# Retention attention into a highway layer: a planner's order replaced by one written-out order of all engines

## The chip, the cores and the metric

The kernel runs on one core of a Trainium2 chip. The metric is the device time of one execution in microseconds; several runs are timed, and their median is given. A profile is one execution recorded by the hardware profiler. Engine names: PE is TensorE (matmul), DVE is VectorE, ACT is ScalarE, POOL is GpSimd, SP is the engine that issues most DMAs.

## The reference

Four sequences of 768 tokens, 8 heads of 64 dimensions. The attention has no softmax; it decays by a per-head `lam` and is computed here in blocks of 64 tokens:

```
intra = (q k^T * Dmask) v          Dmask[i,j] = lam^(i-j) for i >= j, else 0
inter = (q * lam^(i+1)) kv_state
out   = intra + inter
kv_state = lam^64 * kv_state + (k * lam^(63-j))^T v
```

The result, as x of 3072 tokens by 512 features, goes through a highway layer with two 512x512 weights:

```
H = relu(x w_h);  T = sigmoid(x w_t + b_t);  y = T*H + (1-T)*x
```

Inputs and output are float32.

## The kernel before

A tile n is 256 tokens of one sequence with all 8 heads, so there are N = 12 tiles, three to a sequence, each of two chunks b of C = 128 tokens. A partition holds two neighbouring tokens (j = 0, 1), so a loaded row piece is 512 bytes. Decay is split into powers by position: v is multiplied by lam^(-position) when it is cast to bf16 (`scale_v`, POOL), and what comes out of attention is multiplied by lam^(+position) (`decay`, DVE, with a table `pow_q` of 128 x 4 x 768 that ACT makes with eight Exp).

Per tile: `load` k, q, v (SP); `cast` k and q to bf16 (POOL) and `scale_v`; `trans`, 8 PE transposes each of k and q; `evac_k`, `evac_q` copy them from PSUM to SBUF (ACT), where `evac_q` puts even and odd tokens back in order; `scores`, 64x64 matmuls for two halves u; `mask` (DVE) multiplies by the triangle into bf16; `state` adds k^T v of a chunk to the running state in PSUM, and `evac_s` copies the state to bf16; `inter` multiplies q by the state and `intra` the masked scores by v, both into `o`; `decay` turns `o` into `xT`, features on partitions. Then the highway layer: `block` is a group of 8 matmuls of 128x128 by 256 tokens for h (w_h) or t (w_t), for a pair of feature blocks; `hmx` is relu(h) - x (DVE), `sigm` the sigmoid (ACT, into bf16 SBUF), `thmx` their product (DVE); `turn` transposes x and adds the product on PE, giving tokens on partitions; `evac_o` copies to SBUF (ACT) and `store` writes 256 KB per chunk (SP). The last tile goes through the highway layer chunk by chunk. The first tile is loaded and cast in two head halves.

What sets the order: every piece of work is a `Task` with an engine, a guessed duration and a key. `plan` runs a list scheduler over them at build time and emits the instructions in the order of its guessed start times; each engine then executes its own part in that order and waits by semaphores. PSUM: two banks for the scores, two for `o`, one for the state, and three that rotate under the tag "w" for everything else (`WB = 3`). The state tile holds each head's 64x64 in its half of the partitions, 256 wide. Weight loads are eight DMAs of 256 KB whose keys place them after tile 0's loads:

```
a = task("SP", 0.5, WA[w] - 0.1 + 0.01 * (w * KC + kc), lambda w=w, kc=kc: load_w(w, kc), size=0.70)
```

Of the kernel before, what the change touches and what calls it, by code (L numbers as in the profile page):

```python
# [10 lines left out]
I32 = mybir.dt.int32  # L11
# [4 lines left out]
class Tile:  # L16
    def __init__(self, tag, bufs):
        self.tag, self.bufs, self.users, self.writers, self.obj, self.old = tag, bufs, [], [], None, None


class Task:
    def __init__(self, emit, eng, dur, key, reads=(), writes=(), after=(), lat=0.08, size=0.0, mode=0, only=()):
        self.__dict__.update(eng=eng, dur=dur, emit=emit, key=key, lat=lat, size=size, mode=mode, only=only)
        self.reads, self.writes, self.after = list(reads), list(writes), list(after)
        self.start = self.done = None


def plan(tasks):

    for t in tasks:  # L30
        deps = list(t.after)
        for x in t.reads:
            deps += [w for w in x.writers if w in t.only] or x.writers
            x.users.append(t)
        for x in t.writes:
            deps += x.writers
            x.users.append(t)
        for x in t.writes:
            x.writers.append(t)
        t.deps = [d for d in deps if d is not t]  # L40
    rings = {}
    engines = {}
    for t in tasks:
        engines.setdefault(t.eng, []).append(t)
    for e in engines.values():
        e.sort(key=lambda t: t.key)
    free = {e: START.get(e, 0.0) for e in engines}
    last_mode = None
    dma_free, services = 0.0, []
    busy = []  # L50
    warm = [False]
    order = []
    live = {}
    turn = {}
    for t in tasks:
        for x in t.writes:
            if x.writers[0] is t and x.tag != "w":
                turn.setdefault(x.tag, []).append(x)

    def slot_time(t):  # L60

        at = 0.0
        for x in t.writes:
            if x.old is None and x.writers[0] is t:
                q = live.setdefault(x.tag, [])
                if x.tag in turn and turn[x.tag][0] is not x:
                    return None
                if len(q) >= x.bufs:
                    prev = q[len(q) - x.bufs]
                    for u in prev.users:  # L70
                        if u.done is None:
                            return None
                        at = max(at, u.done if u.eng != t.eng else u.done - u.lat)
        return at

    def ready(t):
        at = slot_time(t)
        if at is None:
            return None
        for d in t.deps:  # L80
            if d.done is None:
                return None
            at = max(at, d.done if d.eng != t.eng or d.eng == "SP" else d.done - d.lat)
        return at

    remaining = len(tasks)
    W = 3.413
    win_end, win_busy, clock = W, 0.0, 1.9
    while remaining:
        best = None  # L90
        for e, ts in engines.items():
            if not ts:
                continue
            cand = None
            fixed = e == "SP"
            seen = 0
            for t in ts:
                r = ready(t)
                if r is not None:
                    s = max(free[e], r)  # L100
                    if cand is None or s < cand[0] - 1e-9:
                        cand = (s, t)
                        if s <= free[e] + 1e-9:
                            break
                seen += 1
                if seen > 60:
                    break
            if cand and (best is None or cand[0] < best[0] - 1e-9):
                best = (cand[0], cand[1], e)
        if best is None:  # L110
            stuck = [(e, ts[0].key) for e, ts in engines.items() if ts]
            raise RuntimeError(f"stuck {stuck}")
        s, t, e = best
        engines[e].remove(t)
        for x in t.writes:
            if x.writers[0] is t and x.old is None:
                live.setdefault(x.tag, []).append(x)
                x.old = True
                if x.tag in turn:
                    turn[x.tag].pop(0)  # L120
        t.start = s
        d = t.dur
        if e == "PE":
            while s >= win_end:
                if win_busy > 0.8 * W:
                    clock = 1.0
                elif win_busy < 0.1 * W:
                    clock = 1.9
                win_end += W
                win_busy = 0.0  # L130
            d = d * clock + (0.1 if t.mode != last_mode else 0.0)
            last_mode = t.mode
            win_busy += d
        t.end = s + d
        free[e] = t.end
        t.done = t.end + t.lat
        if e == "SP":
            begin = max(dma_free, s + 1.4)
            if len(services) >= 2:
                free[e] = max(free[e], services[-2])  # L140
            services.append(begin)
            dma_free = begin + t.size
            t.done = dma_free + (1.6 if t.writes or not t.reads else 0.4)
        order.append(t)
        remaining -= 1
    order.sort(key=lambda t: t.start)
    return order


LAT = dict(PE=0.25, ACT=0.08, DVE=0.08, POOL=0.08, SP=0.0)  # L150
START = dict(PE=4.8, ACT=6.2, DVE=4.9, POOL=4.2, SP=0.75)
W_ENG = ["POOL", "DVE"] * 4
LA = 5
XB = 3
OB = 12
WB = 3
KQ, KK, KV, KI, KS, KF, KO, KST = 0.9, 0.8, 0.6, 0.45, 0.5, 1.2, 1.8, 3.0
WA = (1, 1)
# [3 lines left out]
def kernel(  # L162
# [25 lines left out]

    def half(e):
        return slice(64 * e, 64 * e + 64)  # L190


    lam_bc = singles.tile([128, H], F32)
    nc.scalar.dma_start(out=lam_bc, in_=lam.partition_broadcast(128))
    bt_r = singles.tile([KC, 128], F32)
    nc.scalar.dma_start(out=bt_r, in_=moe_b_t.rearrange("(j p) -> j p", p=128))
    id128 = singles.tile([128, 128], BF16)
    make_identity(nc, id128)

    tri = singles.tile([128, J, C], F32)  # L200
    nc.gpsimd.memset(tri, 1.0)
    for b in range(2):
        nc.gpsimd.affine_select(out=tri[half(b)], in_=tri[half(b)], compare_op=ALU.is_ge, fill=0.0, base=0,
                                pattern=[[-1, J], [1, C]], channel_multiplier=-J)

    tk_i = singles.tile([128, NST, J], I32)
    nc.gpsimd.iota(tk_i, pattern=[[-2 * C, NST], [-1, J]], base=0, channel_multiplier=-J)

    tq_i = singles.tile([128, S], I32)
    nc.gpsimd.iota(tq_i, pattern=[[1, S]], base=0, channel_multiplier=0)  # L210
    ln_bc = singles.tile([128, H], F32)
    nc.scalar.activation(ln_bc, lam_bc, AF.Ln)
    ln_hp = singles.tile([128, NP], F32)
    for e in range(2):
        nc.scalar.activation(ln_hp[half(e), :], ln_bc[half(e)].rearrange("p (hp e) -> p e hp", e=2)[:, e, :], AF.Copy)
    tk_f = singles.tile([128, NST, J], F32)
    nc.vector.tensor_copy(tk_f, tk_i)
    tq_f = singles.tile([128, S], F32)
    nc.vector.tensor_copy(tq_f, tq_i)
    pk_ln = singles.tile([128, NST, H, J], F32)  # L220
    nc.vector.tensor_tensor(pk_ln, in0=ln_bc[:, None, :, None].to_broadcast([128, NST, H, J]),
                            in1=tk_f[:, :, None, :].to_broadcast([128, NST, H, J]), op=ALU.mult)
    pow_k = singles.tile([128, NST, H, J], F32)
    nc.scalar.activation(pow_k, pk_ln, AF.Exp)
    pow_q = singles.tile([128, NP, S], F32)
    id_f = singles.tile([KC, KC], F32)
    nc.vector.tensor_copy(id_f, id128[0:KC, 0:KC])
    bt_ps = ps.tile([128, KC], F32, tag="w", name="bt_ps", bufs=WB)
    nc.tensor.transpose(bt_ps, bt_r, id_f)
    bt_col = singles.tile([128, KC], F32)  # L230
    nc.vector.tensor_copy(bt_col, bt_ps)
    w_f = [singles.tile([128, KC, DM], F32, name=f"w_f{i}") for i in range(2)]
    w_b = [singles.tile([128, KC, DM], BF16, name=f"w_b{i}") for i in range(2)]
    wh, wt = w_b


    tasks = []
    made = {}

    def buf(name, tag, shape, dtype=BF16, bufs=1, pool=None):  # L240
        made[name] = Tile(tag, bufs)
        made[name].make = lambda: (pool or sb).tile(shape, dtype, tag=tag, name=tag, bufs=bufs)
        return made[name]

    def get(*key):
        x = made[key]
        if x.obj is None:
            x.obj = x.make()
        return x.obj
# [274 lines left out]
```

## Time and profile before

| what | value |
|---|---|
| time, median of 3 runs | 119.48 us (118.65, 119.48, 119.56) |
| profiled execution: span from first to last instruction | 118.0 us |
| profiled execution: time of its own beside the span | not given; the runs lie 0.6 to 1.5 us above the span |
| PE busy | 98.8 us |
| DVE busy | 81.1 us |
| ACT busy | 70.7 us |
| POOL busy | 52.3 us |
| granted PE clock | full in all slices |
| HBM read, written | 20.98 MB, 6.29 MB |

How to read it: the page gives busy time, then forty equal slices of the span in tenths, then the chain of work that ended last. A group line gives source line, engine, operation, output and inputs with shapes, count, busy time and mean duration, and the idle time before it with what released it. A matmul's listed duration holds its pipeline, so four that overlap each show some 220 ns; start to start is what counts.

### The profile page before, as it was taken

What the parts mean: (1) busy time and instruction counts of PE and PEld (TensorE: products, weight loads), DVE (VectorE), ACT (ScalarE), POOL (GpSimd) and SP (SyncE); (2) the same over time, 40 slices, a digit from 0 to 9 for tenths busy, and PEclk for the clock granted to TensorE, in tenths of its full rate; (3) what the DMA queues carried; (4) which work ended last, traced back from release to release, by engine and by line L of the source; (5) the groups of instructions that cost most, each with busy time, mean ns of one, the idle gap of its engine ahead of it and who ended that gap; (6) DMA issues with size and microseconds to landing.
All of it is one profiled execution on the core that took longest, in us unless ns stands there. A gap on an engine that the chain in (4) does not pass through costs nothing.

```text
span 118.0 us, 4685 instructions
## 1 busy us (share of the span) xinstructions
PE 98.8 (84%) x2049; PEld 83.0 (70%) x2049; DVE 81.1 (69%) x138; ACT 70.7 (60%) x135; POOL 52.3 (44%) x52
## 2 busy tenths in 40 slices
PE   0056548776899999999999999999988999999970
PEld 0044436565688878888888888888777888888950
DVE  0539461229768887969869788698698775988460
ACT  3599203393874665784677757837576578353860
POOL 7148432777585765864484647458360000000000
PEclk9999999999999999999999999999999999999999
DMA  0999999899999999999999999999912204004045
GB/s 17 267 304 380 366 294 284 234 252 305 289 293 272 301 290 290 305 300 322 335 290 315 304 265 300 300 315 263 314 64 89 94 0 173 10 6 178 6 178 177
DMA packets 42413, 27.57 MB, mean 234 GB/s; under 512 B 1301, under 2 KB 38425, under 8 KB 42393
## 3 DMA queue, kind: packets, MB, share of 16 engines
q1 hardware_dynamic: 42240, 27.27, 82.4%
q8 instruction: 16, 0.26, 1.0%
q14 instruction: 5, 0.03, 0.1%
q10 hardware_dynamic: 152, 0.01, 0.1%
HBM read 20.98 MB, written 6.29 MB: 231 GB/s over the span
## 4 chain that ended last, share of the span: by engine, by line
PE 67%; DMA 12%; DVE 7%; SPq 4%; issue 3%; ACT 2%; POOL 1%; DVEq 0%
PE w L367 33%; PE w L385 9%; DMA qf<-in_q_dram 8%; PE w L299 8%; PE s L317 6%; PE o L341 5%; DMA w_f<-in_moe_w_h_dram 4%; DVE th L379 4%; SPq L282 4%; PE kv L349 3%; PE o L330 3%; DVE m L321 2%; ACT L376 1%; POOL qb L286 1%; ACT t_sb L376 1%
## 5 line engine op out<-in xcount | busy, mean ns | idle before, releaser
L367 PE MATMUL w<-xT,w_b 128*128 128x256 bf16 (+1 forms) x416 | 49.0, 268 | 0.0
L367 PEld LDWEIGHTS <-w_b 128*128 128x128 bf16 x416 | 36.9, 99 | 4.6
L321 DVE TENSOR_TENSOR m<-s,tri 128x512 bf16<-128x512 f32 x48 | 31.6, 684 | 4.0 <-PE s L317 3.5
L376 ACT ACTIVATE t_sb<-w,bt_col 128x256 bf16<-128x256 f32 (+1 forms) x52 | 21.0, 458 | 18.6 <-PE w L367 17.1
L292 POOL TENSOR_TENSOR vs<-vf,pow_k 128x1024 bf16<-128x1024 f32 (+1 forms) x13 | 23.1, 1778 | 11.7 <-DMA vf<-in_v_dram 9.1
L355 DVE TENSOR_TENSOR xT<-o,pow_q 128x512 bf16<-128x512 f32 x24 | 15.4, 685 | 11.4 <-PE o L341 11.4
L371 DVE SCALAR_TENSOR_TENSOR hmx<-w,xT 128x512 bf16<-128x512 f32 (+1 forms) x26 | 16.7, 642 | 5.5 <-PE w L367 5.4
L286 POOL CAST qb<-qf 128x1024 bf16<-128x1024 f32 (+1 forms) x13 | 12.7, 979 | 16.4 <-DMA qf<-in_q_dram 13.9
L379 DVE TENSOR_TENSOR th<-t_sb,hmx 128x512 bf16<-128x512 bf16 (+1 forms) x26 | 15.8, 606 | 4.7 <-ACT t_sb L376 4.5
L391 ACT ACTIVATE o_sb<-w 128x512 f32<-128x512 f32 (+1 forms) x24 | 13.7, 588 | 7.3 <-PE w L385 7.3
L303 ACT ACTIVATE kT<-w 128x1024 bf16<-128x1024 bf16 (+1 forms) x13 | 12.4, 954 | 6.5 <-PE w L299 6.5
L308 ACT ACTIVATE qT<-w 128x1024 bf16<-128x1024 bf16 x11 | 11.3, 1024 | 7.4 <-PE w L299 7.4
L286 POOL CAST kb<-kf 128x1024 bf16<-128x1024 f32 x11 | 11.9, 1079 | 5.3 <-DMA kf<-in_k_dram 5.3
L385 PE MATMUL w<-id,th 128*128 128x128 bf16 x96 | 13.1, 219 | 0.6 <-DVE th L379 0.6
L385 PE MATMUL w<-id,xT 128*128 128x128 bf16 x96 | 13.2, 220 | 0.0
L317 PE MATMUL s<-qT,kT 64*64 64x128 bf16 x384 | 11.5, 229 | 1.5 <-DVE m L321 1.4
L349 PE MATMUL kv<-vs,kb 64*64 64x64 bf16 x320 | 9.2, 198 | 2.1 <-POOL vs L292 1.4
L349 PEld LDWEIGHTS <-kb 64*64 64x64 bf16 x320 | 7.6, 113 | 4.2 <-issue 4.2
L299 PE MATMUL w<-id,kb 128*128 128x128 bf16 x96 | 8.4, 235 | 2.5 <-POOL kb L286 1.9
L317 PEld LDWEIGHTS <-kT 64*64 64x64 bf16 x384 | 7.5, 110 | 3.9 <-DVE m L321 2.4
L385 PEld LDWEIGHTS <-th 128*128 128x128 bf16 x96 | 9.3, 98 | 1.1 <-DVE th L379 1.0
L385 PEld LDWEIGHTS <-xT 128*128 128x128 bf16 x96 | 9.1, 98 | 1.0
(37 smaller groups left out, 78.3 us busy)
## 6 DMA issues: line engine op xcount, KB each, us to landing
out_dram<-o_sb SPq DMA_DIRECT2D x23, 256.0 KB, 4.8
kf<-in_k_dram SPq DMA_DIRECT2D x11, 512.0 KB, 7.3
qf<-in_q_dram SPq DMA_DIRECT2D x11, 512.0 KB, 7.8
vf<-in_v_dram SPq DMA_DIRECT2D x11, 512.0 KB, 7.1
w_f<-in_moe_w_h_dram SPq DMA_DIRECT2D x4, 256.0 KB, 5.2
w_f<-in_moe_w_t_dram SPq DMA_DIRECT2D x4, 256.0 KB, 5.6
kf<-in_k_dram SPq DMA_DIRECT2D x2, 256.0 KB, 4.7
qf<-in_q_dram SPq DMA_DIRECT2D x2, 256.0 KB, 5.5
```

The source lines that it names most:

```text
L286: eng.tensor_copy(get(x + "b", n)[:, :, hs, :].rearrange("p j h d -> p h j d"), get(x + "f", n, p).rearrange("p h (j d) -> p h j d", j=J))
L292: eng.tensor_tensor(get("vs", n)[:, hs].rearrange("p h j d -> p (h j) d"), in0=get("vf", n, p).rearrange("p h (j d) -> p (h j) d", j=J), i ...
L299: T.transpose(get(x + "tr", n, p)[:, i, j, :], get(x + "b", n)[:, j, h:h + 2, :], id128)
L317: T.matmul(get("s", n, u)[half(b), e, i, j, :], lhsT=get("kT", n)[half(e), hp, j, half(b)], rhs=get("qT", n)[half(e), hp, b * C:(b + 1) * ...
L321: V.tensor_tensor(get("m", n, u)[:, e], in0=get("s", n, u)[:, e], in1=tri[:, None].to_broadcast([128, 2, J, C]), op=ALU.mult)
L349: T.matmul(get("kv", n // NST)[half(e), hp, :], lhsT=get("kb", n)[half(b), j, 2 * hp + e, :], rhs=get("vs", n)[half(b), 2 * hp + e, j, :], ...
L355: V.tensor_tensor(get("xT", g)[:, :, r * C:(r + 1) * C], in0=get("o", n)[:, b], in1=pow_q[:, :, c * C:(c + 1) * C], op=ALU.mult)
L367: T.matmul(get(x, g, js[0])[:, i, :], lhsT=w[:, kc, j * 128:(j + 1) * 128], rhs=get("xT", g)[:, kc, :], start=(kc == 0), stop=(kc == KC - 1))
L371: V.scalar_tensor_tensor(get("hmx", g, js[0]), in0=get("h", g, js[0]), scalar=0.0, in1=get("xT", g)[:, js[0]:js[-1] + 1, :], op0=ALU.max, ...
L376: A.activation(get("t_sb", g, js[0])[:, i, :], get("t", g, js[0])[:, i, :], AF.Sigmoid, bias=bt_col[:, j:j + 1])
L379: V.tensor_tensor(get("th", g)[:, js[0]:js[-1] + 1, :], in0=get("t_sb", g, js[0]), in1=get("hmx", g, js[0]), op=ALU.mult)
L385: T.matmul(get("x", n, b, p)[:, (j - js[0]) * 128:(j - js[0] + 1) * 128], lhsT=get(x, g)[:, j, r * C:(r + 1) * C], rhs=id128, start=(j == ...
```

## The change

The planner, its tasks and their guessed costs are removed. A string `PLAN` lists every step of every engine in one sequence; each token is a step with its tile, half and, where there is a choice, its engine after `@` and its PSUM bank or banks after `=` (seven single banks b0 to b6, the eighth for the state). The kernel walks the string and emits.

```
+PLAN = """
+Lq.0.0 Lq.0.1 Lq.1.0 Lk.0.1 Lv.0.1 Lk.0.0 Lv.0.0 Lk.1.0 CQ.0.1@POOL Lq.1.1 Lv.1.1 CQ.0.0@POOL CK.0.1@ACT Lk.1.1
+TQ.0.0=0 TQ.0.1=1 Lv.1.0 TK.0.1=2 EK.0.1@DVE CK.0.0@POOL Lq.2.1 CV.0.1@DVE TK.0.0=3 EQ.0.1@DVE CV.0.0@POOL Lk.2.0
...
+I.2=61 CQ.3.2@POOL Lk.4.1 X.1.1@DVE G.1.0@ACT A.2.0 A.2.1
+X.0.0@DVE Lv.4.0 TK.3.2=2 D.2.1@ACT H.1.0 R.0.1.2=5 EK.3.2@ACT Lk.5.1 CV.3.2@POOL TQ.3.2=0 X.1.0@DVE R.0.0.2=1 Lq.5.0
+EQ.3.2@ACT D.2.0@DVE R.1.1.2=3 R.1.0.2=4 Lk.5.0 E.0.1.2@ACT CQ.4.2@POOL SS.3.1=26 F.2.1.0=0 Lv.5.0 KE.3.0@ACT M.3.1.1
...
+"""
```

The tokens: L loads, W weight loads, C casts (CQ now a multiply), WC weight casts, T transposes, E with K or Q their copies out of PSUM, SS scores with state (S and U each alone, in tile 0), KE state copy, M mask, I inter, A intra, D output copy into `xT` (`take`), F highway matmuls, H relu, G sigmoid, X gate multiply, R turn, E output copy, ST store. What the steps do differently:

```
+    def cast_q(n, p, eng):
+        scale(n, p, eng, "qf", new(("qb", n), [128, J, H, D])[:, :, heads(p)].rearrange("p j h d -> p h j d"), pow_q)
...
+    def state(n, b, hp, j, e):
+        first = n % NST == 0 and b == 0 and hp == 0 and j == 0
+        T.matmul(kv[half(e), hp, half(e)], lhsT=get("kb", n)[half(b), j, 2 * hp + e, :],
+                 rhs=get("vs", n)[half(b), 2 * hp + e, j, :], start=first, stop=True, skip_group_check=True)
...
+    def scores_state(n, e, bk):
...
+        for i, (hp, j, x) in enumerate((hp, j, x) for hp in range(NP) for j in range(J) for x in range(2)):
+            score(n, e, hp, j, x)
+            if st:
+                state(n, b, *st[i])
...
+                    T.matmul(get("o", n, b)[:, hp, :], lhsT=get("ss", n, b)[:, hp, :],
+                             rhs=get("qT", n)[:, hp, :, half(b)],
+                             start=hp == 0, stop=False, skip_group_check=True)
...
+    def take(n, b, eng):
+        g, r = groups(n, b)
+        z = 2 if len(g) == 1 else 1
+        copy(eng, new(("xT", *g), [128, NP, z * C], tag=f"xT{z}")[:, :, r * C:(r + 1) * C].rearrange("p n (q j) -> p n j q", j=J),
+             get("o", n, b).rearrange("p n (j q) -> p n j q", j=J))
...
+        dst = src if place == "ACT" else new(("tb", g, u), [128, 2, z * C], tag=f"tb{z}")
```

In words. The query's decay power is multiplied in when POOL casts q, from a small table like v's; the 768-wide table and the multiply after attention go, and `take` is a plain copy on ACT or DVE. Tokens stay even-odd through q's copy, the scores, the mask and `o`, and `take` writes them back in order. Scores are made for one head parity e at a time and alternate with the state matmuls of the chunk on the other half of the rows. The state is 128 wide per head pair with zeros off its diagonal (one memset), so `inter` is one full 128x128 matmul per head pair and chunk, and the state copy is 512 wide. The sigmoid is written in place in PSUM and the gate multiply reads it there. Loads are all in head halves of 256 KB, and weights come as four DMAs of 512 KB, after most of tile 2. The sigmoid table is loaded ahead of its first use. All stores are from SP: 256 KB each, the last chunk's in two halves, as before. A step that keeps PE spinning (`Z`) is defined and not used.

## The prediction

> **What bounds the kernel now.** I read the page first: busy shares and the forty slices.
>
> ```profile
> PE 98.8 (84%) x2049; PEld 83.0 (70%) x2049; DVE 81.1 (69%) x138; ACT 70.7 (60%) x135; POOL 52.3 (44%) x52
> PE   0056548776899999999999999999988999999970
> DMA  0999999899999999999999999999912204004045
> ```
>
> From slice 12 on TensorE is full; before that it is half idle while the DMA engines are full. So there are two stages: a start of some 34 us that waits for data, then a stretch that TensorE sets. The chain of waits in order of time shows the end of the start:
>
> ```profile
> 11.18 9.08 DMA qf<-in_q_dram
> 20.31 1.05 POOL qb L286
> 21.41 1.05 PE w L299 x8
> 22.50 1.02 issue
> 23.52 1.28 ACT L376
> 24.81 0.85 ACT t_sb L376 x2
> 25.68 1.29 DVE th L379
> ```
>
> Tile 1's q lands only at 20.3 us, because all 2 MB of weights were queued before tile 1; then a table load of 1.28 us and a slow gate multiply stand on the path. The same chain in a full stretch prices TensorE's pieces:
>
> ```profile
> 55.78 0.55 PE w L299 x8
> ...
> 58.55 0.45 PE w L299 x8
> 58.99 0.87 PE w L367 x8
> 59.87 0.57 PE o L341 x32
> 60.44 0.24 PE kv L349 x16
> 60.68 1.85 PE w L367 x16
> ```
>
> Eight transposes take 0.45 us behind another 128-wide group and 0.55 behind a 64x64 one: a change of array shape costs about 0.1. In the trace four 64x64 matmuls on different quarters start 3 to 4 ns apart and the next four 56 ns later; a pair of state matmuls takes 32 ns; start gaps at a change of shape are about 93 ns longer. The waits and the gate's tile view show the rest:
>
> ```profile
> POOL qb L286 <- DMA qf<-in_q_dram: 13.9, 10, 3.7
> POOL vs L292 <- DMA vf<-in_v_dram: 9.1, 10, 2.0
> ...
> L379 DVE TENSOR_TENSOR th<-t_sb,hmx x26: 283/415/1724, 25.7 to 113.7; 128x512 bf16<-128x512 bf16 x22, 128x256 bf16<-128x256 bf16 x4
> ```
>
> GpSimd (Pool) idles for data; the gate multiply takes 415 ns at the median and up to 1724.
>
> **What the Trainium skill says.** "TensorEngine Tiling (Array Packing)", Key Properties: changing the tiling mode drains the engine. The 0.45 against 0.55 agrees. "SBUF — State Buffer", Who interferes with whom: a Vector instruction with two SBUF inputs shares a port with a Pool instruction that reads SBUF, and the later one waits. The spread 415 to 1724 agrees, as does the mask with one PSUM input, which stays within 673 to 692. "VectorE: DVE Perf Modes", perf-mode tier table: a copy from PSUM runs at up to 2x. No bf16 1024-element Vector copy is in this trace.
>
> **The change part by part.**
>
> *TensorE.* Units, from the spacings above: 8 transposes or 8 output-turn matmuls 0.45, 8 wide F matmuls 0.875, 16 scores 0.225 (four rounds), 32 intra 0.45, 16 state 0.256, 16 inter 0.45. A full tile before: F 3.5, transposes 0.9, turns 0.9, intra 0.45, scores 0.45, state 0.51, inter 0.45, and six changes of shape 0.56: 7.7. The chain's intra groups from 30.08 to 106.81 give 7.67 a tile. After: alternating takes a score pair on one row half and a state pair on the other, so a round of four costs 56 ns; 16 scores with 16 states take 0.45, two of those 0.90, against 0.96. Inter becomes 8 full-array matmuls of 56 ns, 0.45 as before. So alternation and block-diagonal state are worth next to nothing by themselves. The written order has 40 changes of shape where the trace has 68: 28 x 0.093 = 2.6 us saved. Summed over all tiles (the first of a batch has half an inter, the last half a state): 90.3 before, 88.2 after.
>
> *Start.* Loads are reordered: tiles 0 and 1 whole, most of tile 2, then weights in four 512 KB pieces between tile 2 and 3. Same bytes, 72 loads of 256 KB where there were 39. The trace lands the first six halves at 5.5 to 10 us and 6.5 MB by 27.3 (v of tile 2); I take 0.93 us per 256 KB and 1.4 per weight piece. Then tile 1 is complete at 15.5, v of tile 2 at 23.9, the last weights at 27.6, tile 3 at 32. Pool's order: the scaling of tile 2's v runs 23.9 to 25.8. The scores-and-state pair of tile 2 therefore ends at 26.9; the 12 us of TensorE work ahead of it fit well before. Then four F blocks 3.5, inter, intra, transposes and four turns of tile 0 and 1; Vector is as late (four masks 2.6, four gates 2.6, relu and copies to 34.1), and v of tile 3 is scaled at 34.1. Tile 3's scores start at 34.4. At that point 18.6 of the 88.2 are done, 69.6 remain. Before, at 34.1, 13.4 of 90.3 were done and 76.9 remained; it took until 114.4, 80.3: 3.4 of waits, 4%.
>
> *The rest of the start.* Eight Exp for the decay table (4.4 us of ScalarE) and its iota go; a memset of the state bank and a second 0.24 Exp come, and the sigmoid table is loaded early, off the path. All this lies beside the first loads: nothing; uncovered, under 1 us.
>
> *Pool.* q's cast (1046 ns) becomes a multiply like v's (1912): 12 x 0.87 = +10 us, 4.9 a tile against some 7 of TensorE, hidden behind the data waits above, which stood at 23. It is not hidden at tiles 2 to 4, where loads arrive every 5.6: included in 34.4; without that cover +0.9 a tile. Loads keep 4 to 7 us ahead of the transposes after tile 4 at 0.295 MB/us.
>
> *Stores.* 25 stores, 6.29 MB, as before: nothing in themselves. But on SP's fixed queue nine stand ahead of the last load, and the one of tile 3's first half is asked for at about 53.4, just when its turn is due: 0 to 2 us of loads held up, covered by that lead.
>
> *Vector and ScalarE.* Removed: 24 decay multiplies (685). Added: 24 output takes, 13 on ScalarE (0.6) and 11 on Vector (0.65 back to back, as the masks' 1.29 for two). State copies double to 512 wide: 0.38 to 0.6 on ScalarE; 10 of 20 go to Vector at 0.65. Eight whole transposed-tile copies go to Vector: unknown, from 0.66 (632 cycles at 0.96 GHz, an estimate from the named page, 2x) to 1.2 (1x; 128x512 with stride took 0.69); even-odd order makes them contiguous, so I take 0.68. Gates read the sigmoid in PSUM: 0.65 steady instead of 0.41 to 1.7; no port wait. Behind tile 3: masks 36 x 0.645, relu 18 x 0.645 + 4 x 0.4, gates the same, takes 5.9, transposed copies 4.0 (7.1 if slow), state copies 3.9, output copies 2.4: 65.5 us of Vector beside 69.6 of TensorE, 94%. Before, Vector had 63.4 in the 80 us from 35 to 115. This is where the gain will leak. Scores now wait for v too, since states stand between them, and state b=1 waits for its copy on a crowded Vector queue; behind a waiting scores pair stand masks, and behind those intra. Walking tiles 3 and 4 by hand I find 1.9 us of waits in 13.8 (mask and state copy behind relu and gates). I take 8% for the whole stretch, between 4% before and that 13%: 5.6 us.
>
> *Sum.* Start +0.3 (34.4 for 34.1), remaining work -7.3, waits +2.2, end from the last turn to the last store unchanged (3.85): 118.04 - 4.8 = 113.2 span. The page gives a span of 118.0 and no separate time of its execution; the median of the runs shown, 119.48, is 1.4 above it, the lowest 118.65 is 0.6. Carrying 1.4 gives 114.6; in proportion, 114.6.
>
> **The rivals.**
>
> A, faster still: waits at 2 to 3%, because port waits of the gate vanish and the order was written with all engines in view. 34.4 + 71.4 + 3.85 = 109.7, time 111.1. For: TensorE held 99.9% busy from 60 to 80 us before. Against: Vector's 94%.
>
> B, no change: the early order doesn't help. If the F blocks of tiles 0 and 1 start with the last weights and Vector or Pool lag, tile 3 starts at 38; with 10% waits 38 + 76.6 + 3.85 = 118.4, time 119.8. For: DMA is full from 2 us on in both. Against: bytes needed for tile 2 fit by 24.
>
> C, slower: Vector becomes the bound in fixed order. Place: tiles 3 to 11. Each tile TensorE waits w for a mask, state copy or gate queued behind others on Vector that are themselves not ready. The forecast has w = 0.6; from w = 1.35 the span passes 119.2 (the 1% line); at w = 1.6 it is 34.4 + 69.6 + 14.4 + 3.85 = 122.3, time 123.7. For: 94%, slow copies add 3 us; seven single PSUM banks named in advance can't be swapped. Against: ScalarE has only some 53 us in the same stretch, and the copies are split in detail.
>
> D: the alternation doesn't run four wide (row halves do not overlap): each scores-state pair costs 0.6 in place of 0.45, +3.3 us, 118 time. Scores across both row halves already overlap, so this is unlikely; it lies in the range.
>
> **How the numbers follow.** Forecast 0.52, A 0.20, B and D 0.12, C 0.16. About 1% is what a measurement of this kernel can tell from no change. Faster: forecast, A and some of B and D: 0.76; within 1%: 0.09; slower: C with a little of B and D: 0.15. The predicted time is the forecast's, 114.6. Range: low 109.5 (below A's centre, with a start 1 us earlier), high 121.0, into C, leaving about two in ten outside; the slow Vector copies and D's price fall within it.
>
> **What would show it.** Right: tile 3's first scores near 34 us, after F blocks of two tiles and four turns; 40 changes of shape; scores-state groups of 32 in about 0.45; the gate near 0.68 without long ones; whole Vector copies near 0.68; TensorE's small waits on Vector spread over tiles 3 to 11; last turn near 109.5. Wrong: TensorE idle over 1 us a tile on masks or state copies, Pool waits for data beyond tile 5, transposed copies of 1.2 on Vector, or a first F block much later than 20 us.

## The result and the profile after

The changed kernel took 111.95 us (median; 111.24 to 112.56) against 119.52 us for the kernel before: a ratio of 0.942, 95% interval 0.9345 to 0.9495, 5.8% faster. The ratio compares undisturbed executions only, so it is not the quotient of the two medians. The forecast was 114.6. The profiled execution took 111.24 us with a span of 109.5, the fastest of the four; the forecast span was 113.2.

The page of the changed kernel: busy time and share by engine, then tenths of 40 slices for TensorE, Vector and the DMA engines.

```profile
span 109.5 us, 4558 instructions
PE 95.4 (87%) x1969; PEld 84.8 (77%) x1969; DVE 84.0 (77%) x144; ACT 66.3 (61%) x120; POOL 60.8 (55%) x51
PE   0007887999999999999999999999999999999960
DVE  0204794739996699799999899899999968867870
DMA  0999999999999999999999999999955331020584
```

TensorE starts later than before (slice 4 instead of 3) and is full from slice 8 instead of slice 12. Vector, at nine tenths or more in 8 of 40 slices before, is there in 19 now.

The list of waits of the changed kernel, TensorE alone (microseconds in total, times, longest; gaps below 0.15 us are not listed), complete:

```profile
PE bqtr L205 <- POOL qb L191: 8.8, 2, 8.3
PE kv L222 <- ACT ss L103: 0.7, 1, 0.7
PE bktr L205 <- POOL kb L105: 0.6, 1, 0.6
PE bx L328 <- DVE th L319: 0.3, 1, 0.3
PE bs L217 <- DVE qT L105: 0.3, 1, 0.3
PE kv L222 <- DVE ss L105: 0.2, 1, 0.2
```

Of the first line 8.3 us are the time until the very first transposes. After 20 us TensorE waited once, for 0.3 us. Busy time in stretches, with the columns TensorE, its weight loads, Vector, ScalarE, Pool, clock, DMA share and GB/s:

```profile
20.00:36.00 16.00, 16.00 (x294) 13.95 (x289) 12.20 (x21) 9.81 (x17) 11.30 (x10) 1.00 1.08 300
36.00:60.00 24.00, 24.00 (x529) 21.04 (x522) 22.60 (x37) 16.21 (x30) 17.88 (x12) 1.00 1.10 306
60.00:80.00 20.00, 20.00 (x468) 17.99 (x465) 18.68 (x31) 12.59 (x23) 15.44 (x11) 1.00 1.08 324
```

Vector was 94% and 93% busy in the last two stretches, and TensorE has no listed wait in them. The gate multiply, in its tile view of the changed kernel (shortest, median, longest in ns):

```profile
L319 DVE TENSOR_TENSOR th<-bt,hm x26: 414/680/693, 30.2 to 105.5; 128x512 bf16<-128x512 f32 x22, 128x256 bf16<-128x256 f32 x4
```

Its longest went from 1724 to 693 ns. Marks on TensorE, in us from the first instruction, place the gain (start times in the two traces; these two executions lie 8.3 us apart, the ratio stands for about 7):

| mark | before | after | gain so far |
|---|---|---|---|
| 64th F matmul (two tiles' worth) | 38.7 | 31.6 | 7.1 |
| first scores of tile 3 | 39.1 | 35.6 | 3.5 |
| last intra of tile 5 | 60.2 | 55.5 | 4.7 |
| last intra of tile 8 | 83.3 | 78.4 | 4.9 |
| last turn | 114.2 | 106.1 | 8.1 |

Between tiles 5 and 8 both kernels go at about the same pace, 23 us for three tiles. The gain is made before 55 us, and again after 83. Of the 3.2 us after 83 only some 0.7 us are known waits: the kernel before stood 0.45 us at a gate of 1.67 us and 0.26 at a mask behind it. Most of the rest, about 2 us by the count of the next paragraph, is work that the changed kernel has already done at that mark, and fewer changes of shape.

Counted in the prediction's unit prices (an estimate), the kernel before has 71.9 us of TensorE work left at tile 3's first scores and takes 75.1 to its last turn; the changed kernel has 69.6 left and takes 70.5. So the 8.1 us are 3.5 at the start, 2.3 of less work behind it and 2.3 of fewer waits.

The chain of the changed kernel in order of time shows a stretch of the full part:

```profile
43.30 1.85 PE bt L301 x16
45.15 0.45 PE bo L272 x8
45.59 0.87 PE bh L301 x8
46.47 0.45 PE bktr L205 x8
46.91 0.87 PE bh L301 x8
47.79 0.45 PE bqtr L205 x8
```

Six groups stand in a row with the array in one shape (the inter group, L272, is now 128 wide too), and the eight transposes take 0.45 us both times; behind a 64x64 group they took 0.55.

### The profile page after: what moved, and what is told of

It is laid out like the page before. It is cut to its first block, busy times and chain, and to the rows that moved or that the text cites. A ratio compares the mean times of both kernels' runs of the same rounds, so it can differ in the third digit from the quotient of the medians.

```text
span 109.5 us, 4558 instructions
## 1 busy us (share of the span) xinstructions
PE 95.4 (87%) x1969; PEld 84.8 (77%) x1969; DVE 84.0 (77%) x144; ACT 66.3 (61%) x120; POOL 60.8 (55%) x51
## 4 chain that ended last, share of the span: by engine, by line
PE 80%; SPq 5%; DMA 5%; DVE 2%; POOL 2%; ACT 2%; issue 1%; DVEq 0%
PE bt L301 20%; PE bh L301 19%; PE bx L328 9%; PE bs L217 8%; PE bo L282 6%; PE bqtr L205 6%; SPq L173 5%; PE bktr L205 5%; DMA qf<-in_q_dram 5%; PE bo L272 5%; PE kv L222 2%; POOL qb L191 2%; DVE o L105 1%; ACT ss L103 1%; ACT o L103 1%
## 5 line engine op out<-in xcount | busy, mean ns | idle before, releaser
L256 DVE TENSOR_TENSOR m<-bs,tri 128x512 bf16<-128x512 f32 x48 | 31.0, 679 | 4.1 <-PE bs L217 3.9
L315 ACT ACTIVATE bt<-bt,bt_col 128x256 f32<-128x256 f32 (+1 forms) x52 | 22.0, 431 | 8.5 <-PE bt L301 5.6
L191 POOL TENSOR_TENSOR qb<-qf,pow_q 128x1024 bf16<-128x1024 f32 (+1 forms) x13 | 23.0, 1772 | 7.0 <-ACT pow_v L134 3.6
L301 PE MATMUL bh<-xT,w_b 128*128 128x256 bf16 (+1 forms) x208 | 25.1, 269 | 0.0
L191 POOL TENSOR_TENSOR vs<-vf,pow_v 128x1024 bf16<-128x1024 f32 (+1 forms) x12 | 22.0, 1835 | 5.5 <-DMA vf<-in_v_dram 5.5
L301 PE MATMUL bt<-xT,w_b 128*128 128x256 bf16 (+1 forms) x208 | 24.0, 265 | 0.0
L319 DVE TENSOR_TENSOR th<-bt,hm 128x512 bf16<-128x512 f32 (+1 forms) x26 | 16.6, 644 | 2.0 <-ACT bt L315 1.2
L306 DVE SCALAR_TENSOR_TENSOR hm<-bh,xT 128x512 bf16<-128x512 f32 (+1 forms) x26 | 16.2, 640 | 1.3 <-PE bh L301 1.3
L217 PE MATMUL bs<-qT,kT 64*64 64x128 bf16 x384 | 15.4, 233 | 0.3 <-DVE qT L105 0.3
L328 PE MATMUL bx<-id,th 128*128 128x128 bf16 x96 | 12.9, 219 | 0.3 <-DVE th L319 0.3
```

What stands on the lines that cost most here:

```text
L191: ENG[eng].tensor_tensor(dst, in0=get(src, n)[:, heads(p)].rearrange("p h (j d) -> p h j d", j=J), in1=pw[:, n % NST, heads(p), :, None].t ...
L217: T.matmul(get("s", n, e, hp // 2)[half(b), hp % 2, j, :], lhsT=get("kT", n)[half(e), hp, j, half(b)], rhs=get("qT", n)[half(e), hp, :, ha ...
L256: V.tensor_tensor(new(("m", n, e, u), [128, 2, J, C]), in0=get("s", n, e, u), in1=tri[:, None].to_broadcast([128, 2, J, C]), op=ALU.mult)
L301: T.matmul(t[:, r, :], lhsT=w_b[w][:, kc, (2 * u + r) * 128:(2 * u + r + 1) * 128], rhs=get("xT", *g)[:, kc, :], start=(kc == 0), stop=(kc ...
L306: V.scalar_tensor_tensor(new(("hm", g, u), [128, 2, z * C], tag=f"hm{z}"), in0=get("h", g, u), scalar=0.0, in1=get("xT", *g)[:, 2 * u:2 * ...
L315: A.activation(dst[:, r, :], src[:, r, :], AF.Sigmoid, bias=bt_col[:, 2 * u + r:2 * u + r + 1])
```

## The experiments

Times of the experiments are given as ratios to the kernel before, run on the same chip; the changed kernel's is 0.942. A ratio divided by 0.942 says how it stands to the changed kernel; the intervals are about one per cent to each side, so differences below that are not read. In a quoted text, "before" is the kernel before.

**Load order undone.** In the changed kernel the four weight pieces stand right behind tile 0:

```
- Lq.1.0 Lk.0.1 Lv.0.1 Lk.0.0 Lv.0.0 Lk.1.0 ... W.0.1 Lk.2.1 W.0.0 ... W.1.1 Lk.3.1 W.1.0
+ Lk.0.1 Lv.0.1 Lk.0.0 Lv.0.0 W.0.1 W.0.0 W.1.1 W.1.0 Lq.1.0 Lk.1.0 ...
```

> The changed kernel with its load order undone: all four weight pieces stand right behind tile 0's loads, ahead of tile 1; nothing else moves. Theory: TensorE, which ran without a gap from 14.4 us, now waits for tile 1 about 5 us; 3 to 5 us slower than the changed kernel, 115 to 117 us. Rival (the first stage is set by the half clock of TensorE and not by data): at most 1 us slower, below 113.

Measured: 0.9752 (0.9652 to 0.9851), 116.83 us; 3.5% slower than the changed kernel, some 4 us. Its waits:

```profile
PE bqtr L206 <- POOL qb L192: 15.3, 2, 9.1
```

Of the 15.3 us, 6.2 are ahead of tile 1's transposes, where the changed kernel waits 0.5, and tile 3's scores start at 39.8 us instead of 35.6. In the written order, then, loading tile 1 and most of tile 2 ahead of the weights is worth about 4 us.

**Load order alone, on the kernel before.** `WA = (1, 1)` becomes `WA = (1.35, 2.2)`, which queues w_h behind tile 1 and w_t behind tile 2's q.

> The kernel before with one part of the change alone: the weights are queued later (w_h after tile 1, w_t after q of tile 2), the planner does the rest. Theory (about half of the gain is the start, in which tile 1 waited behind 2 MB of weights): 3 to 4 us faster than before, 115.5 to 116.5 us, first scores of tile 3 some 3 us earlier than 34. Rival (the start was bound by bytes whatever their order): within 1% of before, 118.5 to 120.5.

Measured: 1.0028 (0.9994 to 1.0063), no gain. Tile 0's highway blocks are done earlier (32nd F matmul at 27.0 us, 29.8 before), but the 64th still starts at 38.4 (38.7 before): in the planner's order those of tile 1 come no sooner. Tile 3's first scores start at 38.6 us; the 34 of the expectation is a misreading, in the kernel before they start at 39.1. In some runs, the profiled one among them (from 19.9 to 23.3 us), the granted TensorE clock was halved for a while, but runs with a mean clock of 0.996 or more took 118.83 to 119.64 us, and one 121.06, so that does not hide a gain. The theory fell: with the planner's order the later weights bring nothing.

**Sigmoid back in SBUF.** In the changed kernel:

```
-        dst = src if place == "ACT" else new(("tb", g, u), [128, 2, z * C], tag=f"tb{z}")
+        dst = new(("tb", g, u), [128, 2, z * C], tag=f"tb{z}")
```

> The changed kernel with the sigmoid written to bf16 in SBUF instead of in place in PSUM, so that the gate multiply has two SBUF inputs as before. Theory: the gate takes 0.42 us when Pool is quiet and up to 1.9 when a Pool multiply holds the port, 0.7 or more in the mean over the tiles up to 80 us; Vector is at 95% there, so TensorE gets waits of 1 to 3 us, 113 to 115. Rival (the shorter gates make up for it): within 0.7 us of the changed kernel.

Measured: 0.9847 (0.9667 to 1.0027), in four runs of 116.52 to 119.40 us; 4.5% slower than the changed kernel, with a wider interval than the others. This one edit takes back most of the gain. The time lines of its Vector (gates alone) and then of its Pool (start, duration, instruction):

```profile
30.04 1.02 DVE L320 TENSOR_TENSOR th<-tb,hm 128x512 bf16<-128x512 bf16 x1 [0.68 <-ACT tb L316]
...
31.58 3.96 DVE L320 TENSOR_TENSOR th<-tb,hm 128x512 bf16<-128x512 bf16 x2
...
36.24 1.34 DVE L320 TENSOR_TENSOR th<-tb,hm 128x512 bf16<-128x512 bf16 x1
```

```profile
29.74 1.04 POOL L106 CAST kb<-kf 128x1024 bf16<-128x1024 f32 x1 [0.45 <-DMA kf<-in_k_dram]
31.31 1.90 POOL L192 TENSOR_TENSOR qb<-qf,pow_q 128x1024 bf16<-128x1024 f32 x1 [0.53 <-PE bt L302]
33.17 2.08 POOL L192 TENSOR_TENSOR vs<-vf,pow_v 128x1024 bf16<-128x1024 f32 x1
35.22 2.08 POOL L192 TENSOR_TENSOR qb<-qf,pow_q 128x1024 bf16<-128x1024 f32 x1
```

Two gates take 3.96 us together, as long as the two Pool multiplies beside them, and end at 35.54, 0.3 us behind the second (35.25); the next ends at 37.58, again 0.3 behind Pool's multiply (37.30). The turns wait for the gates (2.9 us of TensorE), the scores of tile 3 start at 39.1, and nothing is made up later: the last turn is 5.1 us late. With the sigmoid in PSUM the same four gates, at the same places, take 0.68 us each.

Not all of this execution's delay is the gates'. The clock row of its page (the granted TensorE clock in tenths of full speed, in 40 slices; 9 stands for 90% or more) has a dip:

```profile
PEclk9999999999995899999999999999999999999997
```

From 34.8 to 38.2 us the granted clock was 0.50, and the transposes and turns in it took about 1.2 us longer, by their start spacing (an estimate). But another run, with a mean clock of 1.000, took 117.34 us, more than this one's 116.52, so the loss does not need the dip.

**Sigmoid in PSUM alone, on the kernel before**, and **both parts on the kernel before**: `sigm` writes and `thmx` reads `get("t", g, js[0])`, the planner is told so, `t_sb` goes; the second also has `WA = (1.35, 2.2)`.

> The kernel before with one part of the change alone: the sigmoid is written in place in PSUM and the gate multiply reads it there; the planner places everything as it likes. Theory (the gate's wait for Pool's port is the largest single cause of the gain: undone in the changed kernel it cost some 5 us, mostly at the first gates): the gate multiply stays within 0.70 us in place of up to 1.7, and the kernel before gets 1.5 to 4 us faster, 115.5 to 118. Rival (one of three rotating PSUM banks is now held until the gate is done, and TensorE waits for it): no faster, 119 to 122.

> The kernel before with two parts: sigmoid in place in PSUM, and weights queued after tile 1 and 2. Theory (the later weights gave nothing alone because the first gates then met Pool's multiplies of tiles 2 and 3): together 4 to 6 us faster than before, 113.5 to 115.5, more than the sum of both alone. Rival (the planner's order, with the highway blocks of a tile behind the attention of the next, is what holds it): no better than the sigmoid in PSUM alone, within 1%.

Measured: 1.0063 (1.0027 to 1.0098) and 1.0394 (1.0280 to 1.0507). The gates do become steady, as the tile view of the first shows, but the time does not follow:

```profile
L379 DVE TENSOR_TENSOR th<-w,hmx x26: 425/680/691, 25.7 to 113.4; 128x512 bf16<-128x512 f32 x22, 128x256 bf16<-128x256 f32 x4
```

In the second, a wait that the kernel before did not have stands in the list of waits, highway blocks on a bank that a gate still reads:

```profile
PE w L367 <- DVE th L379: 2.4, 3, 1.7
```

These 2.4 us fit the held bank, the rival named for the first of the two: with three rotating banks a t block keeps its bank until its gate is done; the written order has seven single banks and says which one is reused when. They are not the whole loss. TensorE also waits 1.8 us for two masks near 34 us, and the granted clock was lower in all four runs, 0.967 to 0.984 in the mean; in the profiled one it was 0.50 from 19.3 to 22.7 and from 36.4 to 39.8 us, where the second stretch costs about 1.2 us by the start spacing (an estimate). How the loss divides is open.

The two parts that cost 3.5% and 4.5% when undone bring nothing when each is done alone, and a loss together. What pays is their combination with the written order; how much the order is worth by itself can't be read from these runs.

**Scores and states apart.** In `scores_state` all 16 scores are emitted first, then all 16 states:

```
-            if st:
-                state(n, b, *st[i])
+        for t in st:
+            state(n, b, *t)
```

> The changed kernel with the scores of one head parity and the state matmuls of the other row half no longer alternating: in each group all 16 scores are emitted, then all 16 state matmuls; nothing else moves. Theory as predicted (neighbours overlap only when they alternate in program order): 16 scores of one row half take 0.45 us, then the states 0.26, so +0.26 us in 20 groups: about 5 us slower than the changed kernel, 117. Rival, suggested by the start times in the changed kernel's trace (matmuls on the two row halves advance as two streams that overtake each other): the states run under the scores whatever their order, less than 1 us slower.

Measured: 0.9444 (0.9326 to 0.9562): no difference that can be read, and not the 5 us of my theory. TensorE's time line of this kernel shows why; L218 are scores and L223 states, emitted strictly one after the other:

```profile
36.77 0.47 PE L218 MATMUL bs<-qT,kT 64*64 64x128 bf16 x10
37.02 0.22 PE L223 MATMUL kv<-vs,kb 64*64 64x64 bf16 x2
37.07 0.22 PE L218 MATMUL bs<-qT,kT 64*64 64x128 bf16 x2
37.08 0.23 PE L223 MATMUL kv<-vs,kb 64*64 64x64 bf16 x4
```

State matmuls start while scores that stand ahead of them have not: the two halves of the array's rows run as two streams. A full group's starts span 0.50 us from first to last in this trace, against 0.42 alternating; the theory's 0.45 and 0.26 would have made it 0.7.

**Alternation undone as before.** Each group takes two head pairs' scores on all four quarters, then its states; masks and intra groups are renamed.

> The changed kernel with the alternation undone as the kernel before had it: each group takes the scores of two head pairs on all four quarters, then the 16 state matmuls; masks and intra groups are renamed to match. Theory as predicted (alternation is worth next to nothing: 0.23 + 0.26 against 0.45): 0 to 1 us slower than the changed kernel, 112 to 113. Rival (row halves as two streams let the alternating groups overlap their neighbours, which the four-quarter scores cannot): 2 to 4 us slower.

Measured: 0.9402 (0.9273 to 0.9531), the same as the changed kernel. A group's starts span 0.47 us in its trace, against 0.42 alternating: 1 us in 20 groups, too little to read in these intervals.

**All takes on Vector.** `D.x.y@ACT` becomes `D.x.y@DVE`, 13 times.

> The changed kernel with all 24 takes on Vector, 13 of them moved from ScalarE: 13 x 0.65 = 8.4 us more on Vector. Theory (Vector has only some 5% to spare between 36 and 96 us, and TensorE had no waits because the order keeps just inside that): about 9 takes fall in the stretch, 6 us of Vector work against some 3 us of slack, TensorE waits 3 to 5 us: 115 to 117. Rival (Vector has slack in the order that its busy share hides): within 1 us of the changed kernel.

Measured: 0.9581 (0.9495 to 0.9666), 113.69 us, 1.7% or about 2 us slower than the changed kernel. Less than expected: Vector had 91.4 us of work in place of 84.0, and only some 2 of the 7.4 reached the end. Its TensorE waits stay small (0.8 for a take, 0.6 for gates); the rest of the loss is not resolved.

**Pool's extra multiply.** `cast_q` is a plain cast again, so this kernel leaves out the query's decay.

> The changed kernel with q's cast as a plain cast again (1.05 us in place of 1.9 on Pool); the query decay is left out. Theory (Pool's extra 10 us is hidden behind data): within 0.5 us of the changed kernel. Rival (Pool is on the path in the start, tiles 2 to 4): 1 to 2 us faster, 110 to 111.

Measured: 0.9424 (0.9343 to 0.9506): nothing, as the theory had it. Pool is busy 50.6 us here and 60.8 in the changed kernel, and those 10.2 us are hidden.

**The end in another order.** F.12.1 before R.10, G.12.1 before E.10.1, H.12.1 and X.12.1 before E.10.0:

```
- F.11.0.0=4 H.11.1 E.9.1.2@ACT R.10.1.2=3 H.11.0 G.11.0@ACT ... R.10.0.2=5 X.11.1@DVE F.12.1.1=1 E.10.1.2@ACT X.11.0@DVE F.12.1.0=2 E.10.0.2@DVE ... G.12.1@ACT
+ F.11.0.0=4 H.11.1 E.9.1.2@ACT F.12.1.1=1 H.11.0 G.11.0@ACT ... F.12.1.0=3 X.11.1@DVE G.12.1@ACT R.10.1.2=2 X.11.0@DVE H.12.1 E.10.1.2@ACT R.10.0.2=5 X.12.1@DVE
```

> The changed kernel with its last 40 steps in another order: the last chunk's F blocks come before the turns of tile 10, its sigmoid before tile 10's output copy on ScalarE, its relu and gate before the other output copy on Vector. Theory: the 3.3 us from the last F block to the last turn shrink to about 1.5, since turns and copies fill the wait; 1.5 to 2 us faster than the changed kernel, about 110.2. Rival (the end is set by the last 1 MB of stores): less than 0.5 us.

Measured: 0.9403 (0.9325 to 0.9481), no gain. The expectation had misread the chain: it leaves TensorE at 102.7 us, but TensorE's time line shows turns and F blocks until 104.7, and only 1.2 us from the last F to the last turn. Its chain now passes through a store:

```profile
103.52 0.60 ACT o L104
104.12 0.03 ACT bt L316
104.15 1.83 DMA out_dram<-o
105.98 0.66 DVE o L106
106.64 0.02 issue
106.66 0.42 DVE oh L106
```

From the turn at 101.1 us (100.3 in the changed kernel's trace) TensorE needs 5.3 us to its last turn instead of 5.8, but from there to the end it is 4.6 us instead of 3.5. What was won at the gate was lost on the copies and stores behind it, as the rival said.

**TensorE warmed up.** Identity matmuls, results unused, ahead of the first transposes (`Z.70=6`) and ahead of tile 1's (`Z.16=0`); then the 70 alone.

> The changed kernel with 70 matmuls of 128x128 on the identity put before TensorE's first transposes and 16 more before those of tile 1, results unused. Theory: TensorE ran at half rate until 23.5 us (128-wide matmuls 107 ns apart, later 56) because it had not been busy enough; warmed up it does the work from 14.4 to 23.4 in half the time and then waits for weights and v of tile 2, so tile 3's scores start about 1 us earlier: 0.5 to 1.3 us faster, 110.7 to 111.5. Rival (rate falls back between the early gaps, or data sets the start): no difference within 0.5 us.

> The changed kernel with the 70 idle matmuls ahead of TensorE's first transposes, without the 16 before tile 1's, which had run at half rate and pushed tile 1 by 1.3 us. Theory (weights and v of tile 2 set the start, not TensorE's rate): 0.3 to 0.8 us faster than the changed kernel, about 111.4. Rival (the 16 cost what the rate had won): 1 to 1.5 us faster, 110.7.

Measured: 0.9335 (0.9225 to 0.9445), 111.62 us, and 0.9579 (0.9503 to 0.9655), 113.73 us. In the first the 70 take 6.5 us: 49 start 107 ns apart, then 56. Tile 3's scores start at 35.1 and 35.5 us, against 35.6. But neither run kept TensorE at its full rate. The clock rows of their pages, the first kernel's and the second's:

```profile
PEclk9999959999999999999999999999999999999998
PEclk9999755599999999999999999999999999999998
```

In the first the granted clock was 0.50 from 13.3 to 16.8 us, in the second from 12.7 to 22.9, and the 128-wide matmuls there start 107 ns apart again. So the second says nothing about a warm TensorE: it did tiles 1 and 2 at half rate like the changed kernel. The first ran them at full rate from 16.8 us on; the scores and state of tile 2 start 0.7 us earlier than in the changed kernel, those of tile 3 0.5. On the way TensorE waited 0.6 us until Pool had multiplied tile 2's q, which the changed kernel did not have to: as far as this one trace shows, beyond some 0.5 us data sets the start.

The second is slower although it does less. Its TensorE waits from 50 us on begin with

```profile
PE bqtr L206 <- POOL qb L192: 0.8, 1, 0.8
PE bktr L206 <- POOL kb L106: 0.7, 1, 0.7
```

where the changed kernel has none: near 75 and 83 us TensorE waited for Pool, and Pool for loads. All six runs took 113.2 us or more, with a mean clock of 0.946 to 0.966 against 0.995 to 1.000 in the changed kernel's, so it is not the chance of one run. Tile 3's scores are not late, so the half clock before them does not explain it; what slows the loads later is open. The first has the lowest ratio here, but its interval overlaps the changed kernel's; no version is shown to beat it.

## Why the prediction was right or wrong

*Direction and place: right.* The kernel is faster, with the start and the full stretch as the two stages. The measured time lies in the forecast range, 2.65 us below the forecast.

*The term that was mis-sized: the waits, 5.6 us.* The sum had 69.6 us of TensorE work behind tile 3's first scores plus 8% waits. From there to the end of the last F block the units add up to 68.6 (69.6 without the last 0.9 of turns), and the trace has 35.6 to 104.75, 69.1: waits and all, 0.5 us over the units. The step that failed is the one from Vector's 94% to a leak there. Vector was that full (22.60 of 24.00), and TensorE did not wait for it: that is what rival A forecast, with less than A's 2 to 3%. What in the order keeps TensorE from waiting for so full a Vector no run shows. The experiment with all takes on Vector says how near the edge is: 7.4 us more work there cost 2.

*Start: 34.4 forecast, 35.6 measured.* The forecast let tile 2's scores and state end at 26.9, released by v, with TensorE's work ahead of them fitting well before. v was scaled at 24.5 to 26.4, 0.6 later than forecast, but the group ended at 28.0, because the F blocks ahead of it were not done before 27.2; TensorE has no listed wait from 19.3 us on. It ran at half rate until 23.5 us (128-wide matmuls 107 ns apart), which the working did not price; in the first warmed-up kernel the group starts 0.7 us earlier. Behind it the 7.5 us to tile 3's scores are as forecast. The 34.1 that the sum sets beside 34.4 is a time with the work done by then, not the same mark: tile 3's scores start at 39.1 in the kernel before. The size of the loads' part was not separated out in the forecast; undone it is 4 us.

*The gate: the mechanism right, the term missing.* I noted steady gates without port waits and gave that no price, as part of Vector's sum. Undone it costs 4.5%; in the profiled execution 2.9 us of it are TensorE's waits for the gates of tiles 0 and 1. The Trainium skill's "SBUF — State Buffer", Who interferes with whom, states the cause, a Vector instruction with two SBUF inputs against a Pool instruction that reads SBUF. The times of Vector and Pool above agree: the gates end 0.3 us after Pool's multiplies.

*Alternation: right.* Next to nothing, as forecast: 0.42 us for a group against 0.47 in the old grouping, forecast 0.45 and 0.48. The later theory that the two row halves overlap only when emitted in turn fell. Rival D (no overlap) is out.

*Shape changes: 40 forecast, 42 in the trace*, against 68, with gaps of the size assumed. No run isolates them, nor the early sigmoid table (its load stood 1.28 us on the path before), nor the decay moved from the output to q's cast.

*Pool: right*, +8.5 us for +10 and hidden. *Vector's transposed copies: right*, 685 ns for 680, in line with the 2x that the Trainium skill's "VectorE: DVE Perf Modes" allows for a copy from PSUM in its perf-mode tier table. *Takes: too low*, 745 ns on ScalarE for 600 and 725 on Vector for 0.65 back to back, which is about 685 alone; hidden.

*Loads' lead of 4 to 7 us: not shown to be there.* The kernel with 70 matmuls alone used it up near 75 and 83 us, with waits of 0.77 and 0.66 us.

*The sums.* Of the 3.7 us between forecast and measured span, 5.1 come from the waits up to the last F block, and the start took back 1.2; a wait of 0.3 at the last turns and an end that is 0.4 shorter nearly cancel. The remaining 0.2 is the forecast's own: its terms add up to 113.45 and not 113.2, because the kernel before is taken to reach its last turn at 114.4, where the trace has 114.2. In rival C the 1% line is passed at w = 1.26, not 1.35.

## What to carry to other kernels

A gate that reads two SBUF inputs on Vector beside a busy Pool took up to 1.72 us where its median is 0.42, and no busy share shows that. Leaving one input in PSUM kept it at 0.68 us in both kernels, but the time fell only with the written order. Parts of a change that are each worth several per cent when undone can be worth nothing when done alone, so undoing a part measures its worth in that order only. A second engine at 94% is no proof of waits: walk which results are needed when. Read the clock row of every profile before explaining a delay: four of the experiments above had a stretch at half clock in the very part that was to be explained.

## What the hardware showed unexpectedly

- 64x64 matmuls on different row halves of the array overtake each other: emitted apart, 16 scores and 16 states start within 0.50 us, the first states ahead of the last six scores; alternating, within 0.42.
- TensorE stayed at half rate (107 ns for 128 columns) for 9 us of transposes, 64x64 groups and one F block with a single wait of 0.7 us, from 14.4 to 23.5 us, while the page's clock row showed full rate; with 70 full matmuls in a row it took 5.1 and 4.5 us to come up in two traces.
- Once up, it fell back to 107 ns (128 columns) for 3.4 us and for 10.2 us in these two traces, this time with the clock row at 0.5. The mean clock of all runs is 0.980 to 0.991 and 0.946 to 0.966, and 0.995 to 1.000 in the changed kernel. Why it falls is open.
- Writing every second bf16 element costs extra on ScalarE: the take's 512 elements 745 ns, the state copy's 512 contiguous ones 594. On Vector it is 725 against 684.
